# The bias of the float32 attention heads as four rows of their score product

## Chip, cores and metric

The kernel runs on one core of one Trainium2 chip. The metric is the device time of one execution in microseconds (us).

## What is computed

```python
# attention: batch 4, 8 heads, 576 positions, head size 64; x = relu(s)
scores = q @ k.T / sqrt(64)
bias   = -(cum[:, None] - cum[None, :])          # cum = cumsum(max(s, 0)) along the positions
scores = where(causal, -1e9, scores + minimum(bias, 0))
attn   = exp(scores - max) / (sum + 1e-9);  out = attn @ v
# then two feed-forward layers on 2304 tokens, 512 -> 2048 -> 512
x = prelu(x @ w_in, alpha) @ w_out
x = (h * clip(h + 3, 0, 6) / 6) @ w_out2, with h = x @ w_in2
```

Below the diagonal `cum` never falls, so the bias of query row i and key column j is `cum[j] - cum[i]`, and it can be added in the score product itself.

## The kernel before

Attention of the first 256 positions of a batch and head is a "head" here; the other 320 positions are done later in another form (`Task`). The first two batches (16 heads, as 8 `Pair`s of heads 2i and 2i+1) run ahead of all weights; the third batch (8 heads, pairs 8 to 11) runs between the products of the first feed-forward layer (`moe1`). Only these 24 heads are computed in float32 and only they are touched here. The last batch and all later positions (`Task`, class `Sums`) already hold the sums as four rows of their operands.

The start, `cumulate`: `s` is loaded four times, once for each group of 32 partitions; VectorE clips and scales it, scans it along the positions (the scan also reads a tile of zeros, `zz`, that GpSimd fills), ScalarE rounds it, and VectorE replaces the second and fourth group by what the rounding left out. `cum2` then holds, for all 32 heads, the sums in two parts, once in rows 0 to 63 and once in rows 64 to 127. It is also written to the scratch tensor `cum_d` in HBM (`cum_scratch` in the rows).

While that goes on, `keep_clock` has TensorE multiply a tile of ones, `busy`, ten times into a bank that nothing reads ("unread products"). Two more follow each head's transposes.

A head of a pair, `softmax_a`: two blocks of query rows (128 by 128 keys, 128 by 256 keys) in one PSUM bank `s`. For each block there are three products: `pick` (a column of the identity, so that one head's sums are chosen) against `cum2` for the key's sums; `cum2` against minus `pick` for the query's; and the float32 product of `q` and `k`. The two heads of a pair lie in rows 0 to 63 and 64 to 127 of one tile (`qn`, `kn`), and the products of each use only its 64 rows. VectorE adds the mask and takes the row's extreme (L265), ScalarE takes the exponential (L270), VectorE the reciprocal, GpSimd scales (L274). Then `finish` follows one head behind (`LAG`): three transposes on TensorE (L497), a copy on ScalarE (L498), and the two products with `v` (`pv`, L504 and L505). In a float32 product the trace shows two records of TensorE, in one with rounded operands one.

Each engine works through its own queue in order. The order in the queues is dealt by a scheduler that goes by a model of the instructions' times and by priorities, so an edit at the start can reorder the queues far behind it. All transfers are issued by SyncE (SP), in order; each waits until an earlier one that used the same completion counter has landed. Weights come through it too (`load_unit`, L126: four transfers of 512 KB per unit), and ScalarE, GpSimd and VectorE take each apart into a rounded part and a rest (`split_part`, L146 to L163) before TensorE can use it.

Of the kernel before, what the change touches and what calls it, by code (L numbers as in the profile page):

```python
# [9 lines left out]
F32 = mybir.dt.float32  # L10
F32R = mybir.dt.float32r
AF = mybir.ActivationFunctionType
ALU = mybir.AluOpType
# [33 lines left out]
class Pools:  # L47


    def __init__(self, stack, tc, name, groups, wb=0, side=None):  # L50
        self.of, self.wb, self.cum2, self.sums = {}, wb, None, None
        for i, tags in enumerate(groups):
            pool = stack.enter_context(tc.tile_pool(name=f"{name}{i}", bufs=2, reuse_waits="tile", side=side))
            self.of.update(dict.fromkeys(tags.split(), pool))
# [6 lines left out]
def attention_moe_moe(ctx, tc, qt, kt, qn, kn, vp, s, w_in1, w_out1, alpha, w_in2, w_out2, out):  # L61
# [155 lines left out]
    nc.gpsimd.affine_select(  # L217
        mask[:, MASK:], mask[:, MASK:], pattern=[[-1, P]], compare_op=ALU.is_ge, fill=NEG, base=0, channel_multiplier=1
    )
    pick = const.tile([P, 2, BH], F32R, name="pick")  # L220
    for part in range(4):
        rows = slice(part * BH, (part + 1) * BH)
        for sign in range(2):
            nc.vector.tensor_scalar_mul(pick[rows, sign, :], ident[:BH, :BH], 1.0 - 2.0 * sign)

    def cumulate(pool, first):

        s_sb = pool.tile([P, S], F32, tag="wcv", bufs=WB0, name="s_sb")
        for part in range(4):
            nc.sync.dma_start(s_sb[part * BH : (part + 1) * BH], s)  # L230
        first.load(pool)
        sp = pool.tile([P, S], F32, tag="wcv", bufs=WB0, name="sp")
        nc.vector.tensor_scalar(sp, s_sb, 0.0, 8.0, op0=ALU.max, op1=ALU.mult)
        zz = pool.tile([P, S], F32, tag="wcv", bufs=WB0, name="zz")
        nc.gpsimd.memset(zz, 0.0)
        cum = pool.tile([P, S], F32, tag="wcv", bufs=WB0, name="cum")
        nc.vector.tensor_tensor_scan(cum, sp, zz, initial=0.0, op0=ALU.add, op1=ALU.add)
        cum2 = pool.cum2
        nc.scalar.activation(cum2, cum, AF.Copy)
        for part in (1, 3):  # L240
            rows = slice(part * BH, (part + 1) * BH)
            nc.vector.tensor_tensor(cum2[rows], cum[rows], cum2[rows].bitcast(F32), op=ALU.subtract)
        nc.sync.dma_start(cum_d.rearrange("t b s -> (t b) s"), cum2[:D].bitcast(F32))

    def softmax_a(pool, sides, bh=None, js=None):

        cum2 = pool.cum2

        rows = [(0, slice(0, P), P), (1, slice(P, 3 * P), 2 * P)]
        sc = bank("s")  # L250
        todo = []
        for u, o, w in rows:
            if bh is not None:
                one, minus = (pick[js, sign, bh : bh + 1] for sign in range(2))
                todo.append((sc[:, o], one.to_broadcast([D, P]), cum2[js, :w]))
                todo.append((sc[:, o], cum2[js, u * P : (u + 1) * P], minus.to_broadcast([D, w])))
            todo += [(sc[:, o], q[:, u * P : (u + 1) * P], k[:, :w]) for q, k in sides]
        for i, (dst, lt, r) in enumerate(todo):
            nc.tensor.matmul(dst, lt, r, start=(i == 0), stop=(i == len(todo) - 1))  # L259
        t = pool.tile([P, 3 * P], F32, tag="t", bufs=T0, name="t")  # L260
        m = sm.tile([P, 2], F32, tag="m0", name="m")
        den = sm.tile([P, 2], F32, tag="den", name="den")
        rec = sm.tile([P, 2], F32, tag="rec", name="rec")
        for u, o, w in rows:
            nc.vector.tensor_tensor_reduce(  # L265
                t[:, o], sc[:, o], mask[:, MASK - u * P : MASK + P], scale=-0.125, scalar=BIG,
                op0=ALU.add, op1=ALU.min, accum_out=m[:, u : u + 1],
            )
        for u, o, w in rows:
            nc.scalar.activation(t[:, o], t[:, o], AF.Exp, bias=m[:, u : u + 1], scale=-1.0, accum_out=den[:, u : u + 1])  # L270
        nc.vector.tensor_scalar_add(den, den, 1e-9)
        nc.vector.reciprocal(rec, den)
        for u, o, w in rows:
            nc.gpsimd.tensor_scalar(t[:, o], t[:, o], rec[:, u : u + 1], 1.0, op0=ALU.mult, op1=ALU.mult)  # L274
        return t
# [190 lines left out]
    def keep_clock(busy, n, t=None):  # L466

        hp = bank("h")
        r = busy if t is None else t.bitcast(BF16).rearrange("p (k t) -> p k t", t=2)[:, :, 1]
        for _ in range(n):  # L470
            nc.tensor.matmul(hp[:, : r.shape[1]], busy[:, :P], r, start=True, stop=True)  # L471

    class Pair:


# [2 lines left out]

        def load(self, pool):
            i, self.pool = self.i, pool  # L480
            self.k = pool.tile([P, NA], F32, tag="kraw", bufs=3, name="kraw")
            nc.sync.dma_start(self.k, kn[i, :, :NA])
            self.q = pool.tile([P, NA], F32, tag="qraw", bufs=3, name="qraw")
            nc.sync.dma_start(self.q, qn[i, :, :NA])
            self.v = pool.tile([P, 2, 2, D], F32, tag="vraw", bufs=3, name="vraw")
            for j in range(2):
                nc.sync.dma_start(self.v[:, j], vp[2 * i + j, :, :2, :])

        def scores(self, j):
            js = slice(j * D, (j + 1) * D)  # L490
            return softmax_a(self.pool, [(self.q[js, :], self.k[js, :])], 2 * self.i + j, js)

# [19 lines left out]
    def attention0(pool, pairs, lag, together):  # L512
# [20 lines left out]
                loaded += 1  # L533

        if pairs[0].i == 0:
            keep_clock(pool.busy, 10)
            cumulate(pool, pairs[0])
            loaded = 1
        ahead(1)
# [101 lines left out]

    with ExitStack() as st:
        pool = Pools(st, tc, "att0", ("wcv", "kraw qraw vraw", "t pT"), WB0)
        pool.cum2 = st.enter_context(tc.tile_pool(name="cum2a", bufs=1)).tile([P, S], F32R, name="cum2")
        pool.busy = st.enter_context(tc.tile_pool(name="busy", bufs=1)).tile([P, 512], BF16, name="busy")
        nc.gpsimd.memset(pool.busy, 1.0)
        att = attention0(pool, [Pair(i) for i in range(H)], LAG, 0)
        attend(att, 2 * H + 1, pool)
    with ExitStack() as st:
# [11 lines left out]

        with ExitStack() as st2:
            pool2 = Pools(st2, tc, "atta", ("kraw qraw vraw", "t pT"))
            pool2.cum2 = st2.enter_context(tc.tile_pool(name="cum2b", bufs=1)).tile([P, NA], F32R, name="cum2")
            for j in range(2):
                nc.sync.dma_start(pool2.cum2[j * D : (j + 1) * D].bitcast(F32), cum_d[:, :, :NA].rearrange("t b s -> (t b) s"))
            att = attention0(pool2, [Pair(i) for i in range(H, H + H // 2)], LAG, 1)
            done = 0
            while f < A2_OF:
                sb1()  # L670
                if f >= A2_AT:
                    attend(att, LAG + 1 + (f - A2_AT) * H // (A2_OF - A2_AT))
            next(att, None)
# [139 lines left out]
```

## Time and profile before

| | |
|---|---|
| median of 3 runs | 1041.73 us (1041.44 to 1043.83) |
| profiled execution | 1042.1 us, its span 1040.3 us |
| TensorE (PE) busy | 1023.4 us, 98% |
| ScalarE (ACT), VectorE (DVE), GpSimd (POOL) busy | 597.7, 542.9, 376.8 us |
| first score product, first weight product, end of the third batch's heads | 8.1, 63.4, 157 us |

The chain of waits follows the work that ended last back to the start; a piece of it is time that nothing else could have filled without a change of order. A busy PE is not a PE at its best: records overlap, and their ends are modelled.

### The profile page before, as it was taken

Reading aid. Unit: us, or ns where it says so; the run is one execution under the profiler, and the core shown is the slowest. Engines: PE = TensorE matmul, PEld = TensorE weight load, DVE = VectorE, ACT = ScalarE, POOL = GpSimd, SP = SyncE. Lnnn points to the kernel's source line nnn. Section 1 sums busy time; section 2 is a strip of 40 time slices with the busy share of each in tenths; the row PEclk is TensorE's granted clock in tenths of the full one; section 3 lists DMA queues with packets and bytes.
Section 4 is the critical chain, followed back from the end, with each engine's and each line's share of the span. In section 5 each row is a group of like instructions: output and inputs, shape, how many; then the busy total and the mean of one; then the engine's idle time right before and its main releaser. Section 6 shows DMA issues by size and latency. Waiting matters only on the chain.

```text
span 1040.3 us, 16822 instructions
## 1 busy us (share of the span) xinstructions
PE 1023.4 (98%) x5930; PEld 878.5 (84%) x5930; DVE 542.9 (52%) x1365; ACT 597.7 (57%) x1326; POOL 376.8 (36%) x515
## 2 busy tenths in 40 slices
PE   8999999899999999999999999999999999999998
PEld 5657788899999998998998888887888888888897
DVE  5468983466666666766664793455422322222222
ACT  4558876877877778787754773565422422322232
POOL 4345745856666666566630540222000000000000
PEclk9999999999999999999999999999999999999999
DMA  5364403302213122213104753300200100000010
GB/s 173 128 222 163 172 1 110 98 27 88 70 50 94 50 74 79 65 50 94 50 13 147 258 196 110 120 1 1 81 1 1 61 1 1 21 21 1 1 41 21
DMA packets 47620, 76.91 MB, mean 74 GB/s; under 512 B 4816, under 2 KB 25520, under 8 KB 47536
## 3 DMA queue, kind: packets, MB, share of 16 engines
q1 hardware_dynamic: 47536, 75.84, 22.5%
q8 instruction: 47, 0.77, 0.3%
q14 instruction: 37, 0.30, 0.1%
HBM read 66.23 MB, written 9.58 MB: 73 GB/s over the span
## 4 chain that ended last, share of the span: by engine, by line
PE 94%; ACT 3%; issue 1%; DMA 1%; DVE 0%; POOL 0%; SPq 0%; ACTq 0%; POOLq 0%; DVEq 0%
PE y L568 19%; PE h L186 19%; PE h L764 19%; PE o L737 13%; PE o L740 6%; PE s L347 4%; PE s L259 4%; PE pt L384 3%; PE pv L409 3%; PE pv L504 1%; PE pt L497 1%; PE h L471 1%; PE pv L505 0%; ACT ks L319 0%; DMA y_scratch<-yt 0%
## 5 line engine op out<-in xcount | busy, mean ns | idle before, releaser
L186 PE MATMUL h<-xhi,wi 128*128 128x256 f32 (+1 forms) x896 | 223.7, 319 | 3.8 <-DVE gt L591 2.2
L764 PE MATMUL h<-yhl,wi 128*128 128x512 f32 (+1 forms) x960 | 213.3, 370 | 0.2
L764 PEld LDWEIGHTS h<-yhl,wi 128*128 128x128 f32 x960 | 169.3, 188 | 34.8 <-DVE gt L767 1.1
L186 PEld LDWEIGHTS h<-xhi,wi 128*128 128x128 f32 x896 | 155.5, 190 | 19.6 <-DVE gt L591 3.1
L568 PE MATMUL y<-gh,wo 128*128 128x256 f32 (+1 forms) x896 | 165.2, 317 | 1.4 <-ACT gh L594 1.0
L766 ACT ACTIVATE gt<-h,three 128x512 f32<-128x512 f32 (+1 forms) x80 | 51.7, 646 | 166.4 <-PE h L764 162.8
L767 DVE SCALAR_TENSOR_TENSOR gt<-gt,h 128x512 f32<-128x512 f32 (+1 forms) x80 | 50.7, 634 | 183.7 <-ACT gt L766 183.3
L737 PE MATMUL o<-wo,gh 128*128 128x512 f32 x576 | 145.8, 391 | 0.1
L568 PEld LDWEIGHTS y<-gh,wo 128*128 128x128 f32 x896 | 133.8, 190 | 13.4 <-ACT gh L594 1.2
L186 PE MATMUL h<-xlo,wi 128*128 128x256 f32 (+1 forms) x448 | 142.3, 318 | 0.0
L737 PEld LDWEIGHTS o<-wo,gh 128*128 128x128 f32 x576 | 106.8, 188 | 22.9 <-ACT gh L770 0.9
L148 POOL TENSOR_SCALAR wcv<-wcv 128x512 f32<-128x512 f32 x64 | 47.2, 746 | 152.4 <-ACT wcv L146 151.3
L568 PE MATMUL y<-gl,wo 128*128 128x256 f32 (+1 forms) x448 | 92.0, 317 | 0.0
L186 PEld LDWEIGHTS h<-xlo,wi 128*128 128x128 f32 x448 | 85.2, 190 | 6.1 <-DVE wcv L156 0.2
L771 DVE TENSOR_TENSOR gl<-gt,gh 128x512 fp32r<-128x512 f32 (+1 forms) x80 | 51.1, 639 | 69.1 <-ACT gh L770 45.6
L359 POOL TENSOR_SCALAR t<-t,rec 128x384 f32<-128x384 f32 (+2 forms) x96 | 65.1, 681 | 60.5 <-DVE rec L358 34.0
L770 ACT ACTIVATE gh<-gt 128x512 fp32r<-128x512 f32 (+1 forms) x80 | 47.3, 591 | 64.0 <-DVE gt L767 32.9
L591 DVE SCALAR_TENSOR_TENSOR gt<-gt,beta,h 128x256 f32<-128x256 f32 (+1 forms) x112 | 61.5, 552 | 39.2 <-ACT gt L590 38.5
L350 DVE CUSTOM_DVE_ANT_0 t<-s,mask 128x384 f32<-128x384 f32 (+2 forms) x96 | 53.8, 563 | 53.7 <-PE pt L384 30.7
L740 PE MATMUL o<-wo,gl 128*128 128x512 f32 x288 | 79.8, 390 | 0.0
L355 ACT ACTIVATE t<-t,m 128x384 f32<-128x384 f32 (+2 forms) x96 | 67.2, 700 | 16.3 <-DVE m L350 15.0
L568 PEld LDWEIGHTS y<-gl,wo 128*128 128x128 f32 x448 | 70.0, 190 | 5.5 <-issue 0.2
(105 smaller groups left out, 1727.5 us busy)
## 6 DMA issues: line engine op xcount, KB each, us to landing
wraw<-in_w_in SPq DMA_DIRECT2D x32, 512.0 KB
wraw<-in_w_out SPq DMA_DIRECT2D x32, 512.0 KB
kraw<-in_kt SPq DMA_DIRECT2D x32, 288.0 KB
qraw<-in_qt SPq DMA_DIRECT2D x32, 160.0 KB
vraw<-in_vp SPq DMA_DIRECT2D x32, 160.0 KB
y_scratch<-yt SPq DMA_DIRECT2D x18, 256.0 KB
yr<-y_scratch SPq DMA_DIRECT2D x4, 1024.0 KB
out<-ot SPq DMA_DIRECT2D x16, 256.0 KB
```

Source lines behind the costliest of these rows:

```text
L186: nc.tensor.matmul(dst, lt, r, start=first and i == 0, stop=last and i == len(terms) - 1)
L350: nc.vector.tensor_tensor_reduce(t[:n, a:e], sc[:n, : e - a], mask[:n, MASK + n - (e - a) :][:, : e - a] if e == w else mask[:n, : e - a], ...
L355: nc.scalar.activation(t[:n, :w], t[:n, :w], AF.Exp, bias=m[-1][:n], scale=-1.0, accum_out=den[:n])
L359: nc.gpsimd.tensor_scalar(t[:n, :w], t[:n, :w], rec[:n], 1.0, op0=ALU.mult, op1=ALU.mult)
L568: nc.tensor.matmul(ys[dc // per][:, o : o + n], which[:, dc * P : (dc + 1) * P], gg, start=(f == 0 and which is wl and dc % per == 0), sto ...
L591: nc.vector.scalar_tensor_tensor(gt, gt, beta[:, f : f + 1], hp[:, :n], op0=ALU.mult, op1=ALU.add)
L737: nc.tensor.matmul(op[i], lt[:, tsl], r, start=(f == 0 and r is wh), stop=False)
L740: nc.tensor.matmul(op[i], gl[:, tsl], wh, start=False, stop=(f == FC - 1))
L764: nc.tensor.matmul(hp[:, :n], lt, r, start=(i == 0), stop=(i == len(terms) - 1))
L766: nc.scalar.activation(gt[:, :n], hp[:, :n], AF.Relu, bias=three)
L767: nc.vector.scalar_tensor_tensor(gt[:, :n], gt[:, :n], 6.0, hp[:, :n], op0=ALU.min, op1=ALU.mult)
L771: nc.vector.tensor_tensor(gl[:, :n], gt[:, :n], gh[:, :n].bitcast(F32), op=ALU.subtract)
```

## The change

The two bias products of a head are left out for pairs 2 to 11; pairs 0 and 1 keep them. From pair 2 on each head lies in rows 4 to 67 of its own half of a tile, and rows 0 to 3 hold the sums: `k` has the two parts of `cum` in rows 0 and 1 and -1 in rows 2 and 3, `q` has 1 in rows 0 and 1 and the two parts in rows 2 and 3. Three pairs of such tiles stand in turn (`Rows`); GpSimd fills rows 0 to 3 once, and with each pair two further transfers bring the sums from `cum_d`. `q` and `k` are loaded from `qt` and `kt` for it, head by head. `pick` moves to a pool of the first stage and is filled by GpSimd instead of VectorE, and the unread products ahead of the first scores are 18 instead of 10. The copy of `cum2` for the third batch is gone.

```diff
@@ Pools
-        self.of, self.wb, self.cum2, self.sums = {}, wb, None, None
+        self.of, self.wb, self.cum2, self.pick, self.sums = {}, wb, None, None, None
@@ before cumulate
-    pick = const.tile([P, 2, BH], F32R, name="pick")
-    for part in range(4):
-        rows = slice(part * BH, (part + 1) * BH)
-        for sign in range(2):
-            nc.vector.tensor_scalar_mul(pick[rows, sign, :], ident[:BH, :BH], 1.0 - 2.0 * sign)
@@ cumulate, after the scan
+        for part in range(4):
+            rows = slice(part * BH, (part + 1) * BH)
+            for sign in range(2):
+                nc.gpsimd.tensor_scalar(pick[rows, sign, :], ident[:BH, :BH], 1.0 - 2.0 * sign, 1.0, op0=ALU.mult, op1=ALU.mult)
         nc.scalar.activation(cum2, cum, AF.Copy)
@@ new
+    R = 4
+    class Rows:
+        def __init__(self, pool, n):
+            self.tiles = []
+            for i in range(n):
+                k = pool.tile([P, 2, NA], F32, name=f"kr{i}")
+                q = pool.tile([P, 2, NA], F32, name=f"qr{i}")
+                nc.gpsimd.memset(k[:R], -1.0)
+                nc.gpsimd.memset(q[:R], 1.0)
+                self.tiles.append((k, q))
@@ Pair.load
-            self.k = pool.tile([P, NA], F32, tag="kraw", bufs=3, name="kraw")
-            nc.sync.dma_start(self.k, kn[i, :, :NA])
-            self.q = pool.tile([P, NA], F32, tag="qraw", bufs=3, name="qraw")
-            nc.sync.dma_start(self.q, qn[i, :, :NA])
+            if i < 2:
+                self.k = pool.tile([P, NA], F32, tag="kraw", name="kraw")
+                nc.sync.dma_start(self.k, kn[i, :, :NA])
+                self.q = pool.tile([P, NA], F32, tag="qraw", name="qraw")
+                nc.sync.dma_start(self.q, qn[i, :, :NA])
+            else:
+                self.k, self.q = pool.rows.tiles[i % 3]
+                both = slice(2 * i, 2 * i + 2)
+                nc.sync.dma_start(self.k[R : R + D], kt[both, :D, :NA].rearrange("j d n -> d j n"))
+                nc.sync.dma_start(self.q[R : R + D], qt[both, :D, :NA].rearrange("j d n -> d j n"))
+                nc.sync.dma_start(self.k[: R // 2], cum_d[:, both, :NA])
+                nc.sync.dma_start(self.q[R // 2 : R], cum_d[:, both, :NA])
@@ Pair.scores
+            if self.i >= 2:
+                return softmax_a(self.pool, [(self.q[: R + D, j], self.k[: R + D, j])])
@@ attention0
-            keep_clock(pool.busy, 10)
+            keep_clock(pool.busy, 18)
@@ first stage
+        pool.rows = Rows(ahead, 3)
@@ third batch
-            pool2.cum2 = st2.enter_context(tc.tile_pool(name="cum2b", bufs=1)).tile([P, NA], F32R, name="cum2")
-            for j in range(2):
-                nc.sync.dma_start(pool2.cum2[j * D : (j + 1) * D].bitcast(F32), cum_d[:, :, :NA].rearrange("t b s -> (t b) s"))
+            pool2.rows = Rows(st2.enter_context(tc.tile_pool(name="rows", bufs=1)), 3)
```

How the queues stand, at three places. GpSimd at the start, before, from the identity to the first head's scaling (`zz` is the scan's tile of zeros):

```order
masks.py:199 AFFINE_SELECT ident_73<-ident_73 128x128
L646 MEMSET busy_122 128x512
L217 AFFINE_SELECT mask_86<-mask_86 128x128
L235 MEMSET zz_149 128x576
L274 TENSOR_SCALAR t_171<-t_171,rec_174 128x128
L274 TENSOR_SCALAR t_171<-t_171,rec_174 128x256
```

And now (`kr0` to `qr2` are the three pairs of tiles):

```order
masks.py:199 AFFINE_SELECT ident_73<-ident_73 128x128
L480 MEMSET kr0_111 4x512
L481 MEMSET qr0_112 4x512
L480 MEMSET kr1_115 4x512
L481 MEMSET qr1_116 4x512
L480 MEMSET kr2_119 4x512
L481 MEMSET qr2_120 4x512
L670 MEMSET busy_126 128x512
L217 AFFINE_SELECT mask_86<-mask_86 128x128
L236 TENSOR_SCALAR pick_110<-ident_73 32x32 x8
L229 MEMSET zz_161 128x576
```

Six fills stand ahead of `busy`, on which the unread products wait, and these and the eight `pick` operations ahead of `zz`, on which the scan waits.

TensorE from the end of the third head's scores, before (`s_262` and `s_293` are the third and fourth head, `t_171` the first head's softmax):

```order
L259 MATMUL s_262<-kraw_157,qraw_159 128x256
L497 MATMUL pt_210<-ident_73,t_171 128x128 x3
L471 LDWEIGHTS busy_122
L471 MATMUL h_215<-t_171,busy_122 128x384
L471 LDWEIGHTS busy_122
L471 MATMUL h_215<-t_171,busy_122 128x384
L259 MATMUL s_293<-cum2_118,pick_91 128x128
```

And now, from the end of the fourth head's (`t_191` is the first head's softmax, `kr2` and `qr2` are pair 2):

```order
L256 MATMUL s_313<-kraw_177,qraw_179 128x256
L518 MATMUL pt_230<-ident_73,t_191 128x128
L256 MATMUL s_352<-kr2_119,qr2_120 128x128
L256 MATMUL s_352<-kr2_119,qr2_120 128x256
L256 MATMUL s_379<-kr2_119,qr2_120 128x128
L256 MATMUL s_379<-kr2_119,qr2_120 128x256
L518 MATMUL pt_230<-ident_73,t_191 128x128 x2
```

Four heads' scores instead of three now precede the first transpose, and both heads of pair 2 stand between the first transpose and the second.

SP around the write of the sums, before (`wraw` are weights):

```order
L482 DMA kraw_202<-in_kn 128x256
L243 DMA cum_scratch<-cum2_118 64x576
L484 DMA qraw_204<-in_qn 128x256
L487 DMA vraw_206<-in_vp 128x128 x2
L126 DMA wraw_218<-in_w_in1 128x2x512
L126 DMA wraw_220<-in_w_out1 128x1024
```

And now:

```order
L500 DMA kr2_119<-in_kt 64x2x256
L501 DMA qr2_120<-in_qt 64x2x256
L506 DMA vraw_226<-in_vp 128x128 x2
L126 DMA wraw_238<-in_w_in1 128x2x512
L126 DMA wraw_240<-in_w_out1 128x1024
L241 DMA cum_scratch<-cum2_109 64x576
L126 DMA wraw_242<-in_w_in1 128x2x512
L126 DMA wraw_244<-in_w_out1 128x1024
L500 DMA kr0_111<-in_kt 64x2x256
L501 DMA qr0_112<-in_qt 64x2x256
L500 DMA kr1_115<-in_kt 64x2x256
L502 DMA kr2_119<-cum_scratch 2x2x256
```

The write stands behind the first two weight transfers, and pair 2's rows are read back behind two more and three loads of `q` and `k`.

## Rows read from the trace of the kernel before

**Rows 1.** The page, part 4: share of the span by engine.

```profile
PE 94%; ACT 3%; issue 1%; DMA 1%; DVE 0%; POOL 0%; SPq 0%; ACTq 0%; POOLq 0%; DVEq 0%
```

**Rows 2.** Chain in order of time, 0 to 230: start us, us, what.

```profile
8.08 5.73 PE s L259 x22
...
15.28 3.74 PE s L259 x15
...
21.96 2.43 PE s L259 x8
...
34.50 0.62 PE h L471 x2
...
40.94 1.30 PE s L259 x8
...
48.54 0.68 PE h L471 x4
...
53.09 0.57 PE pv L504 x2
53.88 0.48 PE pt L497 x3
...
77.61 1.30 PE s L259 x8
```

**Rows 3.** Timeline of the start: start us, us, engine, line [idle before].

```profile
1.70 0.53 POOL L646 MEMSET busy<- 128x512 bf16 x1
...
2.28 4.45 PE L471 MATMUL h<-busy 128*128 128x512 bf16 x10 [2.28 <-POOL busy L646]
...
2.40 0.58 POOL L235 MEMSET zz<- 128x576 f32 x1
...
5.17 1.36 DVE L237 TENSOR_TENSOR_SCAN cum<-sp,zz 128x576 f32<-128x576 f32 x1
```

**Rows 4.** Timeline of PE, 36 to 42 us: one head's scores.

```profile
38.77 0.32 PE L259 MATMUL s<-cum,pick 64*128 64x128 f32 x1
...
39.05 0.44 PE L259 MATMUL s<-kraw,qraw 64*128 64x128 f32 x2
39.24 0.36 PE L259 MATMUL s<-cum,pick 64*128 64x256 f32 x1
...
39.55 0.59 PE L259 MATMUL s<-kraw,qraw 64*128 64x256 f32 x2
```

**Rows 5.** Stretches: length, busy us of PE, PEld, DVE, ACT, POOL, granted clock, DMA.

```profile
0.00:75.00 75.00, 69.82 (x316) 44.40 (x317) 39.98 (x145) 39.79 (x113) 31.11 (x65) 1.00 0.54 173
75.00:130.00 55.00, 55.00 (x267) 41.93 (x266) 48.77 (x102) 45.33 (x91) 35.07 (x46) 1.00 0.47 170
```

**Rows 6.** Stretches between 470 and 484 us, columns as in the group before.

```profile
475.00:478.80 3.80, 1.93 (x13) 1.12 (x13) 2.27 (x8) 3.73 (x12) 3.35 (x4) 0.99 0.24 60
478.80:482.10 3.30, 3.30 (x14) 3.28 (x15) 1.80 (x10) 3.25 (x10) 2.17 (x4) 0.50 0.39 122
```

**Rows 7.** GpSimd's groups by shape, 0 to 160: busy us, mean ns | idle before.

```profile
L274 POOL TENSOR_SCALAR t<-t,rec 128x128 f32<-128x128 f32 x24 | 12.5, 520 | 37.6 <-DVE rec L272 17.2 <-DVE m L265 9.5 <-PE pv L505 6.0
...
L286 POOL MEMSET kb<- 4x256 f32 x2 | 0.6, 302 | 0.0
...
L104 POOL MEMSET three<- 128x1 f32 x1 | 0.1, 100 | 0.0
```

**Rows 8.** Groups of instructions, 0 to 100 us: ScalarE's part of a head.

```profile
L270 ACT ACTIVATE t<-t,m 128x128 f32<-128x128 f32 (+1 forms) x40 | 17.7, 445 | 8.4 <-DVE m L265 8.3
...
L498 ACT ACTIVATE pT<-pt 128x384 f32<-128x384 f32 x18 | 8.8, 487 | 8.2 <-PE pt L497 8.0
...
L270 ACT ACTIVATION_READ_ACCUMULATOR t<-t,m 128x1 f32 x40 | 7.5, 188 | 0.0
```

**Rows 9.** Timeline, 10 to 19 us: the fourth weight transfer and its first reader.

```profile
11.66 0.47 SPq L126 DMA_DIRECT2D wraw<-in_w_out  x1
...
18.58 0.67 ACT L146 ACTIVATE wcv<-wraw 128x512 f32<-128x512 f32 x1 [0.47 <-DMA wraw<-in_w_out]
```

## What was predicted, before the changed kernel had run

> **What bounds the kernel now.** I read the chain that ended last first: PE carries 94% of the span [rows 1]. So an edit is worth what it takes off PE in the stretch where PE is late, less whatever is late next. The chain in order of time [rows 2] then shows the stage that the change touches. The reader is to compare two pieces of equal work there: one head's eight score records take 2.43 us at 21.96 and 1.30 us at 40.94. Likewise two unread products take 0.62 us at 34.50, while four take 0.68 us at 48.54. Nothing in the kernel differs between these pieces; TensorE runs at the lower of its two levels (1.2 GHz) until about 34.8 us and at the higher (2.4 GHz) from there. The clock column doesn't say so: it reads 1.00 for 0 to 75 us [rows 5], so here the durations decide.
>
> Third comes the start [rows 3]: GpSimd fills `busy` at 1.70, ten unread products run from 2.28 for 4.45 us (0.445 each, the lower level), and PE then stands until the sums are there, at 8.08. The scan starts at 5.17, so 2.91 us pass from its start to the first score product. Last, the granted clock at 475 to 482 us [rows 6]: after 3.8 us in which PE was busy for 1.93, it reads 0.50 for 3.3 us of full work, then 1.00 again. A thin stretch costs the higher level, and dense work brings it back.
>
> **The start.** Six fills of 4x512 now stand ahead of `busy` on GpSimd, eight `pick` operations come over from VectorE, and `zz`, which the scan reads, stands behind them. A fill of 4x256 took 0.302 us [rows 7] and one of 128x576 0.58 [rows 3], so 512 columns take some 0.53: six are 3.2 us. `busy` then ends at 1.70 + 3.2 + 0.53 = 5.4, and the 18 products start there. A 32x32 `pick` operation has no row on GpSimd. It lies between 0.100 us (one column filled) and 0.520 us (the same kind of operation on 128 columns) [rows 7], so eight cost 0.8 to 4.2 us. I take 0.25 each, 2.0, since by columns it is nearer to the small one. With 0.2 for the mask (between the end of `busy`, 2.23, and 2.40 [rows 3]) the scan can start at 5.4 + 0.2 + 2.0 + 0.58 = 8.2 and the scores at 8.2 + 2.91 = 11.1 (9.9 to 13.3). The 18 products end at 5.45 + 8.0 = 13.4 if all run at 0.445, at 11.5 if half of them run at the higher level. I take 11.5: the scores start **3.4 us later** (2 to 5.3). VectorE loses eight small operations; it was waiting there, so that is worth nothing.
>
> **The level.** Ten products in 4.45 us did not raise the clock, and a gap followed. 3.3 us of full work did raise it at 482 [rows 6]. Eighteen products, up to 8 us with no gap to the scores, should. Then the 26.7 us from 8.08 to 34.8, which the chain gives to PE nearly without a break, shrink by 1.30/2.43 to 14.3: **12.4 us less**. The bounds are 0 (not raised) and 13.
>
> **The products removed.** Heads of pairs 2 to 7 (twelve heads) lose both bias products of both row blocks. At the higher level these take, from start to start, 39.05 - 38.77 = 0.28 and 39.55 - 39.24 = 0.31 us [rows 4]: 0.59 of 1.30 per head, 7.1 us in all. The float32 product, with 68 rows for 64, I take at its old price: on 256 columns it shows 0.59 us in two records [rows 4], and `pv`, which contracts 128 rows over 256 columns, also takes two records and 0.57 [rows 2]. Against this stands a loss. Two heads in a row ran partly beside each other while one lay in rows 0 to 63 and the other in 64 to 127: three heads took 5.73 us at 8.08, where three times 2.43 are 7.29, and at 15.28 two took 3.74 instead of 4.86 [rows 2]. From pair 2 on both heads of a pair start at row 0. In the old order only one such meeting lies among them (15.28), so I give back 1.1 x 0.535 = 0.6: **6.5 us less**. The Trainium skill, "TensorE: Matmul & The Clock Gate", Part 3, says that small-K products in distinct row groups run concurrently and gives 3.07 times for four tiles of K=32; two K=64 heads would then by its logic come up to twice as fast as apart. By that rule the merged form would give nothing back wherever heads meet; the rows show 1.3 times, and few meetings.
>
> **New waits.** By now PE needs 4 x 1.30 + 12 x 0.71 for scores and, for 16 heads, 0.48 (transposes) + 0.34 (unread) + 0.79 (`pv`, from 53.09 to 53.88) [rows 2]: 39.5 us from 11.5 on. Two things are late next. (a) PE's queue now has four heads' scores, one transpose, and then pair 2, which needs rows of `cum_scratch`. On SP its write now waits behind two weight loads and for VectorE, two more weight loads follow, and only then come the reads. A weight load issued at 11.66 had landed only at 18.58 [rows 9]; the reads, issued some 3 us after the sums, I expect at 17 to 18, where PE would be ready at 16: 1.8 us (0 to 4). The issues themselves, two more per pair at some 0.47 us each, fit between the pairs. (b) ScalarE spends 2 x (0.445 + 0.188) + 0.487 = 1.75 us per head [rows 8], 28 in all, of 39.8 busy up to 75 us [rows 5]. So it is nearly as full as PE, and waits between the two can't all be hidden. Of PE's 39.5 us I take 10%, 3.9 us (0 to 7). Together **5.7 us more**. GpSimd's six fills for the second batch (3.2 us) stand ahead of weight conversions that are due a dozen us later; I take them at nothing, and at 3 us if they were not hidden.
>
> **The second batch.** Eight heads among the first weight stage lose 0.59 each (one takes 1.30 at 77.61 [rows 2]): 4.7 us. VectorE is busy there for 48.8 of 55 us [rows 5], converting weights, so I count half: **2.4 us less** (0 to 4.7).
>
> **Later stages** keep their work, but the order is dealt anew far down the program: 0, give or take 3.
>
> Sum: 3.4 - 12.4 - 6.5 + 5.7 - 2.4 = -12.2. The profiled execution took 1042.1 us (span 1040.3), 0.4 above the median of the runs, so **1030**; its own range is 1025 to 1036.
>
> **Rivals.** *The level is raised and lost again.* From 12 to 18 us PE has scores for four heads and then waits for the first softmax and pair 2. At 475 a stretch half idle was enough to lose it [rows 6]. Against it: PE here has 3 to 4 of 6 us to do. At the lower level a head costs (0.71 + 1.61)/0.535 = 4.3 for 2.3 us, so three heads until it is back cost 6 us: 1036. The same page of the Trainium skill, Part 4, says that the full clock does not engage for transposes, which don't count as busy the same way; that would favour this rival, since transposes are what PE has then. No row here separates them.
>
> *The weights give it back.* The first weight stage can't run ahead of its conversions; VectorE at 89% [rows 5] becomes the bound, and of the 9.8 us won before it 3 to 5 survive, with nothing of the second batch: 1038. Against it: VectorE is busy for only 40 of the first 75 us.
>
> *Slower: the level isn't raised at all before the weight products.* Place: the unread products, which come 3.1 us later and must do what ten didn't. Then the start costs 3.4, the wait 1.8, and four heads save 4.4 up to 34.8, so PE is about level there; but eight heads follow at 4.3 us each instead of 3.0 at the higher level, 10 us, less 2.4: 1050. It decides from three such heads on; with fewer the removed products pay for it.
>
> *Softmax bounds the heads, and a faster PE only waits.* Then ScalarE's work would set the length. Its 39.8 us up to 75 [rows 5] are what PE needs here, so all of (b), 7 for 3.9: 1033.
>
> **How the numbers follow.** The forecast holds with 0.58, the lost level 0.15, the weights 0.13, not raised 0.08, softmax 0.06. A measurement of this kernel can tell 0.3%, 3.1 us, from no change, so faster is below 1038.6. That gives 0.57 of the forecast, 0.10 of the lost level, 0.06 of the weights and 0.05 of softmax: 0.78. Same gets 0.12, mostly the weights and the lost level; slower 0.10, the third rival and a bad deal of the later order. The range runs from 1022 (early start, little waiting, all of the second batch) to 1041.
>
> **What would show it.** In the changed profile the last unread products should take 0.22 us each, not 0.445; the first score record should stand at 11 to 12; a head of pair 2 or later should take 0.7 us; the first weight products (63 us before) should come at 52 to 55; and the gain should stand by 75 us and grow by some 2 us by 130. The forecast is wrong if records of equal work are twice as long again after 18 us, if GpSimd's fill of `zz` ends after 9.8, or if PE stands for more than 4 us ahead of the first product of pair 2.

## The result, and the profile after

| | us |
|---|---|
| before, beside the changed kernel | 1042.78 median of 4 (1041.44 to 1044.06) |
| changed kernel | 1027.97 median of 4 (1027.47 to 1029.26) |
| ratio | 0.986, 95% interval 0.9842 to 0.9878 |
| changed kernel, profiled | 1028.13, span 1026.4 |

1030 was forecast, 1022 to 1041; the change is 14.8 us faster where 12.2 was said. In the later series the executions of the kernel before, five slow ones near 1053 left out, fall into two groups, near 1035.7 and between 1041 and 1045, and the four beside the changed kernel were all of the upper group. So 14.8 is the gain over that group; over the lower one it is some 8, and over both together the changed kernel's ratio was 0.9891 (0.9853 to 0.993), some 11 us. Below, kernels are compared with one another by their medians, and the kernel before stands for its upper group. The changed kernel gave 1028.0 and 1028.2 in two series.

PE's share of the chain (page, part 4) is 92% where it was 94% [rows 1]:

```profile
PE 92%; ACT 2%; DVE 2%; DMA 1%; POOL 1%; issue 1%; SPq 0%; ACTq 0%; POOLq 0%; DVEq 0%
```

The start of the changed kernel, as [rows 3] (start us, us, engine, line; in brackets the idle time before and what ended it):

```profile
4.51 0.51 POOL L670 MEMSET busy<- 128x512 bf16 x1
...
5.08 6.40 PE L468 MATMUL h<-busy 128*128 128x512 bf16 x18 [5.08 <-POOL busy L670]
...
5.46 1.76 POOL L236 TENSOR_SCALAR pick<-ident 32x32 fp32r<-32x32 f32 x8
...
7.28 0.58 POOL L229 MEMSET zz<- 128x576 f32 x1
...
7.90 1.36 DVE L231 TENSOR_TENSOR_SCAN cum<-sp,zz 128x576 f32<-128x576 f32 x1 [2.55 <-POOL zz L229]
...
9.33 0.15 PEld L468 LDWEIGHTS <-busy 128*128 128x128 bf16 x1 [0.28 <-issue]
...
9.75 1.23 PEld L468 LDWEIGHTS <-busy 128*128 128x128 bf16 x6 [0.28 <-issue]
...
10.78 0.51 SPq L241 DMA_DIRECT2D cum_scratch<-cum  x1
...
11.41 0.32 PE L256 MATMUL s<-cum,pick 64*128 64x128 f32 x1
```

The reader is to see the weight loads of the unread products: one each 0.43 us up to 9.33, then six in 1.23 from 9.75. There the level rises, and the scores start at it, 3.33 us later than before. (As in the kernel before, the clock column reads 1.00 from the start on, so here too the durations decide.) But the level doesn't hold. The same kernel by stretches (length, busy us of PE, PEld, DVE, ACT, POOL, granted clock, DMA share, GB/s), as [rows 5, 6]:

```profile
0.00:75.00 75.00, 62.36 (x298) 40.53 (x299) 45.31 (x153) 44.71 (x127) 45.53 (x91) 0.91 0.63 209
75.00:130.00 55.00, 54.99 (x264) 44.45 (x262) 50.84 (x98) 47.49 (x91) 37.55 (x47) 1.00 0.33 122
...
14.00:16.00 2.00, 1.44 (x14) 1.04 (x13) 0.02 (x2) 1.32 (x4) 0.82 (x2) 1.00 0.94 352
16.00:18.00 2.00, 0.05 (x1) 0.05 (x1) 1.32 (x7) 2.00 (x10) 1.53 (x4) 0.67 1.04 391
18.00:20.00 2.00, 0.43 (x1) 0.13 (x1) 1.99 (x8) 1.89 (x9) 1.82 (x4) 0.50 0.40 96
20.00:26.00 6.00, 5.69 (x20) 4.67 (x21) 4.65 (x19) 3.60 (x14) 5.82 (x9) 0.50 0.23 67
26.00:28.00 2.00, 2.00 (x10) 1.05 (x9) 1.52 (x5) 0.96 (x2) 2.00 (x5) 0.77 0.02 5
...
68.00:70.00 2.00, 2.00 (x5) 1.61 (x6) 1.31 (x6) 2.00 (x8) 1.76 (x4) 0.50 0.82 202
...
475.00:482.00 7.00, 7.00 (x59) 7.00 (x58) 3.69 (x16) 5.26 (x16) 4.54 (x7) 1.00 0.10 28
```

PE does next to nothing from 16 to 20 us, the clock falls to 0.50 and comes back only in 26:28. It is at 0.50 once more at 68:70. At 475, where the kernel before lost it [rows 6], PE is now busy throughout and keeps it. Who is waited for at 16 to 20, first on PE and its weight loads, then on ScalarE, then on SP, then along the chain (start us, us, what), all of the changed kernel:

```profile
14.85 0.59 PE L256 MATMUL s<-kraw,qraw 64*128 64x256 f32 x2
17.95 0.47 PE L518 MATMUL pt<-ident,t 128*128 128x128 f32 x1 [2.51 <-DMA wraw<-in_w_out]
...
17.95 0.18 PEld L518 LDWEIGHTS pt<-ident,t 128*128 128x128 f32 x1 [2.91 <-POOL t L271]
...
20.31 2.90 PE L256 MATMUL s<-kr,qr 68*128 68x128 f32 x8 [1.88 <-DMA kr<-cum_scratch]
```

```profile
13.70 0.67 ACT L146 ACTIVATE wcv<-wraw 128x512 f32<-128x512 f32 x1 [3.73 <-DMA wraw<-in_w_in]
15.05 0.66 ACT L146 ACTIVATE wcv<-wraw 128x512 f32<-128x512 f32 x1 [0.68 <-DMA wraw<-in_w_out]
15.62 0.39 ACT L267 ACTIVATE t<-t,m 128x128 f32<-128x128 f32 x1
```

```profile
15.54 0.33 SPq L502 DMA_DIRECT2D kr<-cum_scratch  x1
15.97 0.25 SPq L503 DMA_DIRECT2D qr<-cum_scratch  x1
...
19.64 0.45 SPq L502 DMA_DIRECT2D kr<-cum_scratch  x1
```

```profile
11.96 7.01 DMA wraw<-in_w_out
...
20.31 2.90 PE s L256 x8
...
30.82 0.66 PE s L256 x4
```

Two things stand behind the weights. On ScalarE it is the first exponential (L267), behind two roundings of weights (L146) that wait 4.4 us for their data. So the first softmax is late, and the transpose at 17.95 waits for it: its weight load names GpSimd's scaling (L271), while the transfer that PE's own row names was only in the middle of landing then. On the way through HBM it is the sums of pair 2. SP issues their two reads, of 4 KB each, at 15.54 and 15.97, behind all four weight transfers, the last of which takes 7.01 us (6.92 before [rows 9]). By the times at which the trace's semaphores count up, the reads land at 19.91 and 20.08, 4.4 and 4.1 us after their issue; PE's row at 20.31 names a read too, but the one issued at 19.64 is pair 4's. PE stands 2.51 + 1.88 = 4.39 us. A head from pair 2 on then takes 0.66 us at the higher level, where eight records took 1.30 [rows 2]. The first weight product (L186) starts at 53.6 us, 9.8 earlier than at 63.4, and the last at 618.5, 13.9 earlier than at 632.4:

```profile
L186 PE MATMUL h<-xhi,wi x896: 274/283/796, 53.6 to 618.5; 128*128 128x256 f32 x128, 128*128 128x512 f32 x52
```

In between something is lost. PE of the changed kernel at the hand-over to the third batch:

```profile
63.18 0.39 PE L186 MATMUL h<-xhi,wi 128*128 128x512 f32 x1
64.58 0.89 PE L256 MATMUL s<-kr,qr 68*128 68x128 f32 x4 [1.01 <-DMA qr<-cum_scratch]
66.48 0.92 PE L256 MATMUL s<-kr,qr 68*128 68x128 f32 x4 [1.01 <-DVE m L262]
67.90 0.80 PE L186 MATMUL h<-xhi,wi 128*128 128x512 f32 x1 [0.49 <-DVE gt L612]
```

The third batch's first heads wait for their rows, PE thins out for four us, and the first weight products after it run at the lower level.

### The profile page after: what moved, and what is told of

It reads as the page before. It is cut to its first block, busy times and chain, and to the rows that moved or that the text cites. A ratio compares the mean times of both kernels' runs of the same rounds, so it can differ in the third digit from the quotient of the medians.

```text
span 1026.4 us, 16686 instructions
## 1 busy us (share of the span) xinstructions
PE 1004.1 (98%) x5858; PEld 866.1 (84%) x5858; DVE 535.6 (52%) x1357; ACT 593.6 (58%) x1326; POOL 389.0 (38%) x535
## 4 chain that ended last, share of the span: by engine, by line
PE 92%; ACT 2%; DVE 2%; DMA 1%; POOL 1%; issue 1%; SPq 0%; ACTq 0%; POOLq 0%; DVEq 0%
PE y L589 19%; PE h L786 19%; PE h L186 19%; PE o L759 13%; PE o L762 6%; PE s L344 4%; PE pv L406 4%; PE pt L381 3%; PE s L256 1%; DMA wraw<-in_w_out 1%; PE pt L518 1%; PE pv L525 1%; ACT t L267 0%; DMA wraw<-in_w_in 0%; DMA qr<-in_qt 0%
## 5 line engine op out<-in xcount | busy, mean ns | idle before, releaser
L186 PE MATMUL h<-xhi,wi 128*128 128x256 f32 (+1 forms) x896 | 225.1, 321 | 2.7 <-DVE gt L612 2.1
L186 PEld LDWEIGHTS h<-xhi,wi 128*128 128x128 f32 x896 | 155.9, 190 | 16.6 <-DVE gt L612 3.6
L186 PE MATMUL h<-xlo,wi 128*128 128x256 f32 (+1 forms) x448 | 142.2, 318 | 0.0
L186 PEld LDWEIGHTS h<-xlo,wi 128*128 128x128 f32 x448 | 85.4, 191 | 6.0 <-issue 0.2
L356 POOL TENSOR_SCALAR t<-t,rec 128x384 f32<-128x384 f32 (+2 forms) x96 | 65.7, 685 | 53.2 <-DVE rec L355 25.8
```

Of the source, the lines that this page charges most:

```text
L186: nc.tensor.matmul(dst, lt, r, start=first and i == 0, stop=last and i == len(terms) - 1)
L356: nc.gpsimd.tensor_scalar(t[:n, :w], t[:n, :w], rec[:n], 1.0, op0=ALU.mult, op1=ALU.mult)
```

## The experiments

**e1_before_18**: the kernel before with the longer run of unread products alone.

```diff
-            keep_clock(pool.busy, 10)
+            keep_clock(pool.busy, 18)
```

> The kernel before with 18 unread products instead of 10, nothing else. Theory: the level is worth most of the first stage's gain. Before, the heads from 8.08 to 34.8 us ran at the lower level, 26.7 us that would be 14.3 at the higher; here no head waits for rows of the scratch tensor, so the level, once raised ahead of the first scores, should hold: 8 to 11 us faster than before, 1032 to 1034, with one head's scores at 1.3 us instead of 2.4 from about 9 us on. Rival 1: the level is lost in the first softmax as in the changed kernel (clock column 0.50 from 17.3 to 27.1 us): 2 to 5 us faster. Rival 2: 18 products from 2.28 us don't raise it at all: 1 to 2 us slower, since the last of them end at 10.3 and the scores wait.

1028.52 us (1027.66 to 1030.85; ratio 0.9883, 0.9844 to 0.9922): as fast as the whole change, and faster than was expected. The level is there from the first scores at 8.5 us, though this kernel too loses it for a while. A rounding of weights on ScalarE (L146) waits 3.33 us for its data, up to 15.48, the exponentials behind it are late, and PE does 0.13 of the next 2 us:

```profile
16.00:18.00 2.00, 0.13 (x1) 0.00 (x0) 0.93 (x6) 2.00 (x9) 1.68 (x4) 0.79 1.05 405
18.00:24.00 6.00, 5.88 (x23) 3.79 (x25) 2.55 (x13) 4.53 (x15) 5.49 (x11) 0.50 0.43 135
```

So the removed products, taken together with what came with them, gave nothing that can be measured. Where they went was the question from here on.

**e2_after_10**: the changed kernel with the old ten products.

```diff
-            keep_clock(pool.busy, 18)
+            keep_clock(pool.busy, 10)
```

> The changed kernel with 10 unread products instead of 18. Theory: in the changed kernel the 18 products buy nothing, because TensorE had done four heads' scores by 15.4 us and then stood until pair 2's rows had landed at 20.3, by which time the higher level was lost again (0.50 from 17.3). At the lower level the four heads take some 3.5 us longer and still end before 20.3: the same time as the changed kernel, within 1 us (1028). Rival: the early level is worth what it saves from 11.4 on: 3 us or more slower (1031 or above).

1032.23 us (1029.58 to 1033.92): the rival was right. In this profile even ten products raise the level, at 8.3 us by the trace's clock records (the last weight load comes 0.35 us after the one at 8.05, where the others lie 0.43 apart), and the first scores run at it; in the kernel before ten did not. But PE stands 1.90 us ahead of these scores, and the level is gone at 11.7 (clock 0.53 from 14 to 26 us). Eight more products are worth 4 us to the changed kernel, where they are worth 14 to the old one; it has less work in the stretch that either level prices, and it loses the level at 16.7 us with 18 products too.

**e3_second_only**: the kernel before, with the new form for pairs 8 to 11 alone.

```diff
+            if i < H:
                 self.k = pool.tile([P, NA], F32, tag="kraw", bufs=3, name="kraw")
...
+            else:
+                self.k, self.q = pool.rows.tiles[i % 3]
...
+            if self.i >= H:
+                return softmax_a(self.pool, [(self.q[: R + D, j], self.k[: R + D, j])])
```

> The kernel before with the change in the second batch of heads alone (pairs 8 to 11 from row tiles of their own, the first 16 heads and the ten unread products as before). Theory: eight heads lose 0.59 us of TensorE each, and TensorE is the bound there, so all 4.7 us come off: 1037 to 1038. Rival (as predicted): VectorE, busy for 48.8 of 55 us there, gives half of it back: 1040. Second rival: the six fills on GpSimd and the transfers of the sums at the hand-over cost what the products save: no change.

1039.36 us (1034.48 to 1043.27), ratio 0.9991 (0.9962 to 1.0019): inconclusive, since the kernel before, beside which it ran, spreads over more than that. In its profile the level rose at 24.7 us, in that of the kernel before at 34.8, with the same start. The stretch that the edit touches is a little shorter: 567.7 us from the first weight product to the layer's last (60.7 to 628.4), where the kernel before takes 569.0, although the level fell once more in it.

**e4_sums_early**: the changed kernel with `pick` filled by VectorE as before, and `busy` ahead of the fills for the rows. (The source has the scan's zeros ahead of the fills too; in the queue they came out behind them, at 5.35 us.)

```diff
+            nc.vector.tensor_scalar_mul(pick[rows, sign, :], ident[:BH, :BH], 1.0 - 2.0 * sign)
...
-                nc.gpsimd.tensor_scalar(pick[rows, sign, :], ident[:BH, :BH], 1.0 - 2.0 * sign, 1.0, op0=ALU.mult, op1=ALU.mult)
...
+        pool.rows = Rows(pool.rowpool, 3)
```

> The changed kernel with pick filled by VectorE at the start, as before, and busy ahead of the six fills on GpSimd. The unread products then start at 2.3 instead of 5.1 us, the sums are there at about 9 instead of 11.4, and the scratch tensor is written ahead of the weights and read back behind one weight transfer instead of four. Theory: the late sums and the wait for pair 2 (15.4 to 20.3 us) and the level lost in it (to 27.1) cost the first stage 2.4 + 3 to 4 + 3.2 us: 5 to 8 us faster than the changed kernel, 1020 to 1023, with the clock column at 1.00 through 20 to 27 us. Rival: from 40 us on the chain runs through weight transfers and their conversion, which don't come earlier: 0 to 2 us faster, 1026 to 1028, with a longer stand of TensorE ahead of the first weight products.

1025.15 us (1021.50 to 1028.23), 2.8 less than the changed kernel by the median, between theory and rival; its six runs spread over both. The scores start at 9.50, but 1.70 us of waiting for VectorE lie ahead of them, and the level falls at 12.1 us while PE is busy:

```profile
10.00:12.00 2.00, 2.00 (x17) 1.65 (x17) 1.18 (x8) 0.76 (x3) 0.00 (x0) 1.00 0.54 121
12.00:14.00 2.00, 2.00 (x14) 2.00 (x14) 0.87 (x7) 1.10 (x6) 0.83 (x2) 0.53 0.81 222
14.00:24.00 10.00, 8.93 (x29) 5.59 (x28) 3.75 (x26) 6.83 (x22) 6.27 (x14) 0.50 0.81 224
```

**c1_weights_later** and **b1_before_18_weights_later**: the first weights four steps later, in the changed kernel and in e1's.

```diff
-W_AT = (2, 14)
+W_AT = (6, 14)
```

> The changed kernel, with the first weights asked for and taken apart four steps later (W_AT 6 instead of 2). Theory: in the changed kernel PE stood from 15.4 to 20.3 us because two weight transfers stood on SP ahead of the reads of the sums, and two roundings of weights (L146, 3.7 us of waiting) on ScalarE ahead of the first exponentials; that gap lost the higher level until 27.1. Without them the first product of pair 2 comes at about 17, the level stays at 1.00 from 10 to 30 us, and the time is 5 to 7 us below the changed kernel's: 1021 to 1023. Rival: the weights are then late for their products (53.6 in the changed kernel), VectorE's conversions become the bound, and what is won before 40 us is given back by 75: 0 to 2 us below, 1026 to 1028, or slower. A second rival: the sums' own way through HBM (write at 10.8, landed by 13) is what is late; then the wait before pair 2 stays above 3 us with nothing of the weights in it.

> The kernel before, with 18 unread products and the first weights four steps later; no bias product is removed. Theory: it holds the higher level from about 8 us on and has no gap at 16 to 18; it beats the kernel before with 18 products (1028.5) by 3 to 5: 1024 to 1026. If the removed products are worth their 6.5 + 2.4 us, the changed kernel with the weights later is 4 to 9 us below this one once its 3.4 us of later start are counted; if it is level with this one, the removed products are hidden or paid back elsewhere. Rival: the weights later cost more than the gap, 1028 to 1031.

1036.85 us (1035.91 to 1038.95) and 1033.95 us (1031.15 to 1035.31): 8.7 and 5.4 slower than their parents. My number for both was wrong, and the first rival right in its direction (b1 is slower than even the rival said, and its trace was not taken apart); the mechanism in the first 40 us came out as said. In c1 pair 2 starts at 15.26, and the clock is 1.00 to 40 us. But its weights were asked for only at 27.9. Their conversions on VectorE then stand among the last heads' softmax, and PE stands 6.69 us for it:

```profile
10.00:20.00 10.00, 9.88 (x68) 7.20 (x66) 7.54 (x42) 6.97 (x29) 4.10 (x10) 1.00 0.39 100
20.00:30.00 10.00, 10.00 (x59) 6.60 (x58) 5.01 (x28) 6.97 (x25) 3.84 (x10) 1.00 0.36 91
50.00:60.00 10.00, 2.38 (x8) 0.99 (x7) 9.80 (x25) 4.61 (x13) 6.08 (x6) 0.50 0.24 96
...
57.65 0.47 PE L518 MATMUL pt<-ident,t 128*128 128x128 f32 x1 [6.69 <-POOL t L271]
```

VectorE is busy for 9.80 of the 10 us in which PE has 2.38: the weights' conversions bound this stretch now, and the first weight product comes at 61.8.

**e6_rows_shared**: one set of row tiles for both batches, so no second fills.

```diff
+    rows0 = Rows(right.enter_context(tc.tile_pool(name="rows0", bufs=1, side="right")), 3)
...
-        pool.rows = Rows(ahead, 3)
+        pool.rows = rows0
...
-            pool2.rows = Rows(st2.enter_context(tc.tile_pool(name="rows", bufs=1)), 3)
+            pool2.rows = rows0
```

> The changed kernel, with one set of the tiles for rows 0 to 3 for both batches: the six fills for the third batch, and the wait for their place, are gone. Theory: at 63.6 to 71.3 us the changed kernel lost some 4 us, since the third batch's reads could be issued only after fills at 57.2, landed at 63, and PE thinned out so that the level fell to 0.50 from 68 to 71.3. Without them PE goes from the heads to the weight products without a break, no clock below 1.00 between 60 and 75, and the time is 2.5 to 4 us below the changed kernel's: 1024 to 1025.5. Rival: the weights and their conversions on VectorE are what is late there (L186 waited 0.49 us for VectorE's L612 at 67.9); then 0, within 1 us of 1028.

1025.39 us (1024.79 to 1026.85), 2.6 less than the changed kernel, as expected, and the clock is 1.00 from 60 to 72 us. The waits there are shorter, not gone:

```profile
64.16 0.92 PE L256 MATMUL s<-kr,qr 68*128 68x128 f32 x4 [0.76 <-DVE m L262]
65.58 0.50 PE L186 MATMUL h<-xhi,wi 128*128 128x512 f32 x1 [0.50 <-DVE gt L612]
```

**b3_combined**: e4's start with the fills last of all, e6's tiles and c1's late weights.

```diff
-W_AT = (2, 14)
+W_AT = (6, 14)
...
+                    nc.gpsimd.tensor_scalar(x[:R].rearrange("p j n -> p (j n)"), zz[:R, : 2 * NA], v, v, op0=ALU.min, op1=ALU.max)
...
+            pool2.rows = rows0[0]
```

> A combination meant to beat both: the changed kernel with pick filled by VectorE as before, the tile of zeros and the unread products ahead of the fills of rows 0 to 3, one set of these tiles for both batches, and the first weights four steps later. Theory: start at 8.5 to 9.5 (2 to 3 us less than the changed kernel), no gap before pair 2 and none at 63 to 71 us, the level held: 1028 - 2.5 - 5 - 3 = about 1017, range 1013 to 1021. Rival: the gains cover the same waits and don't add, the first weight stage goes by its conversions on VectorE: 1021 to 1025.

1035.79 us (1034.18 to 1039.26), a plain miss: it is as slow as c1, with the same late weights (first weight product at 66.4 us), and PE stands 3.96 us for the sums of pair 2. The reads that it waits for are the last of six on SP, issued at 15.66 and 15.98 and landed at 17.64 and 17.82; why the order was dealt so was not taken apart.

**n1_weights_behind_sums, n2_before_weights_behind, o1_weights_behind_only**: the first unit's weights neither ahead of the sums nor at 28 us. GpSimd writes one element of each of the four tiles once the first head's reciprocal is there, and the transfers wait for that. n1 is e6 with it, n2 is e1 (all bias products), o1 the changed kernel with nothing else.

```diff
+        if len(recs) < 8:
+            recs.append(rec)
...
+                if after is not None:
+                    nc.gpsimd.tensor_scalar(t[:1, 0, 0:1].bitcast(F32), after[:1, :1], 1.0, 1.0, op0=ALU.mult, op1=ALU.mult)
                 d = nc.sync.dma_start(t.rearrange(
...
-            units.append(load_unit(w_in1, w_out1, len(units)))
+            units.append(load_unit(w_in1, w_out1, len(units), None if units else recs[0]))
```

> The changed kernel with one set of row tiles (as e6_rows_shared) and the first unit's four weight transfers held until GpSimd has scaled the first head's softmax (some 14.5 us instead of 9.4): GpSimd writes one element of each tile first. They then stand on SP behind the reads of the sums for pairs 2 to 4, and their roundings on ScalarE behind the first four heads' exponentials; unlike c1_weights_later, which asked for them only at 27.9, they land at about 22. Theory (the weights ahead of the sums lose the level and 5 us, while weights at 28 us are too late for their products): pair 2 starts at 15 to 16, clock 1.00 from 10 to 60, first weight products at 46 to 51, 4 to 7 us below e6_rows_shared's 1025.4: 1018 to 1021. Rival: the conversions of the weights bound that stage whatever comes before; then first weight products at 53 or later and 1025 or more.

> The kernel before with 18 unread products and the same hold on the first unit's weights as n1_weights_behind_sums; all bias products are there. Theory: the wait at 16 to 18 us and the lower level at 18 to 24 of e1_before_18 (1028.5) go, 1023 to 1026, and the bias products that n1 lacks are what parts the two: n1 is 3 to 7 us below this one (some 11 us of products, less 3 of later start and what the weights' conversions take back). Rival: the removed products are hidden by the conversions; then n1 and this one are within 2 us of each other.

> The changed kernel with the first unit's weights held until the first head's softmax is scaled (as n1_weights_behind_sums), but with its own second set of row tiles and their six fills. Theory: two separate losses, the weights ahead of the sums (2 to 3 us) and the fills ahead of the third batch (2.6 us by e6_rows_shared), add up to the 5 us between the changed kernel (1028) and n1 (1023.2): then 1025 to 1026.5. Rival: the two losses are one (with the heads early, the fills come due while PE still has heads, or with the fills there, what is won is waited away): 1023 or 1028.

> The changed kernel itself once more, beside o1 on the same chip: 1027.5 to 1029.3 as before, if the numbers of the several series may be compared with each other.

| kernel | us | first weight product |
|---|---|---|
| n1 | 1023.17 (1022.45 to 1024.86) | 50.1 |
| n2 | 1028.16 (1027.40 to 1029.00) | 52.1 |
| o1 | **1021.73** (1021.46 to 1021.88) | 48.9 |
| o2, the changed kernel again | 1028.23 (1027.30 to 1029.76) | 53.2 |

o1 is the fastest here, 6.5 us below the changed kernel on the same chip (ratio to before 0.9825, 0.9791 to 0.9859). In its trace SP reads the sums first. Pair 2's reads are issued at 13.19 and 13.62 and land at 14.88 and 15.13, so they take 1.7 and 1.5 us instead of 4.4 and 4.1: of the 5 us by which they came too late in the changed kernel, half was the later issue and half the longer way beside the weights. PE goes from pair 1 to pair 2 without a gap, and the level holds up to 458 us, where it is lost for a while (clock 0.57 from 458 to 462), much as in the kernel before at 479 [rows 6]. SP, PE and stretches of o1:

```profile
13.19 0.33 SPq L508 DMA_DIRECT2D kr<-cum_scratch  x1
...
16.00 0.41 SPq L128 DMA_DIRECT2D wraw<-in_w_in  x1
```

```profile
15.06 0.33 PE L524 MATMUL pt<-ident,t 128*128 128x128 f32 x1
15.26 0.89 PE L260 MATMUL s<-kr,qr 68*128 68x128 f32 x4
...
58.09 0.89 PE L260 MATMUL s<-kr,qr 68*128 68x128 f32 x4
```

```profile
16.00:18.00 2.00, 2.00 (x16) 1.73 (x15) 1.58 (x10) 2.00 (x9) 1.67 (x5) 1.00 0.55 122
...
68.00:70.00 2.00, 2.00 (x10) 1.66 (x9) 1.34 (x3) 2.00 (x4) 0.00 (x0) 1.00 1.05 414
```

The theory of two losses that add up fell: o1 keeps the second fills and is 1.4 us below n1, which doesn't. The fills cost 2.6 us only where the weights stand ahead of the sums; with the heads on time they are covered: in o1 GpSimd makes them from 52.93 to 55.77 us, and the third batch's first scores, at 58.09, show no wait. Why n1 (from another series, and 2 us above its expected range) is slower than o1 wasn't followed further. n2 against e1 says how much the same hold is worth to a kernel that reads no sums early: 0.4 us, where 2.5 to 5.5 were expected, although n2 keeps the level that e1 loses from 17 to 24 us. The reason is open; it may be in part that e1's order lets two heads' scores run beside each other more often (1.85 us for two at 26.62 and at 38.18, where two apart take 2.60).

n1 is 5.0 below n2, with the higher level all through in both: that is the removed products' own gain, net of a start 1.7 us later. From the first scores to the first weight product n1 takes 39.2 us for 42.9 (the forecast had 6.5 of products less and 3.9 of waiting more), and from there to the layer's last product 563.3 for 566.7 (forecast: 2.4 less).

## Why the prediction came out right, and where it was wrong

The chain of kernels takes the 14.8 us apart: before 1042.8; n2 1028.2 (level held, all products, first scores at 9.19 instead of 8.08); o1 1021.7 (products removed, first scores at 10.90); changed 1028.2 (weights ahead of the sums). What waiting is left in o1 stands in the third row.

| term of the sum | forecast | measured |
|---|---|---|
| later start | +3.4 | +3.33 (8.08 to 11.41) |
| the level, if it holds | -12.4 | -15.7 (before to n2 is -14.6, with 1.1 of later start in it) |
| removed products, with the third batch's | -6.5 - 2.4 = -8.9 | -8.1 (n2 to o1 is -6.4, with 1.7 of later start in it) |
| new waits | +5.7 | +6.0 (o1 to changed is +6.5, with 0.5 of later start in it) |

**Right.** The start came out to 0.1 us, and for the reason given: the scores follow the last unread product at 11.41 (forecast 11.5), while the sums were there at 10.76. The pieces came 0.2 to 0.4 us earlier or shorter than said: `busy` done at 5.02 for 5.4, eight `pick` operations 1.76 for 2.0, `zz` done at 7.86 for 8.2. The last unread products take 1.23 / 6 = 0.21 us, a merged head 0.66 for 0.71. The first weight product comes 9.8 us earlier, which is the forecast's 3.4 - 12.4 - 6.5 + 5.7; but only the sum fits, as the next paragraph shows. Heads side by side: the first two now take 11.41 to 13.33, 1.92 us where twice 1.30 are 2.60, so 1.35 times, as the 1.3 that the prediction read from [rows 2]. The Trainium skill, "TensorE: Matmul & The Clock Gate", Part 3, gives 3.07 times for four tiles of K=32. The estimate that the prediction drew from it, up to twice for two heads of K=64, is not reached here.

**The step that failed is (a) of the new waits.** It was put at 1.8 us, for the sums alone, on SP, with the reads landing at 17 to 18 us. Measured are reads that land at 20.08, 4.39 us of standing, and behind it the rival "raised and lost again", which the forecast held apart at 0.15: the records after 20 us are twice as long, eight of pair 2's in 2.90. Two of the three marks by which the forecast called itself wrong are there. What it missed is two things. One is how long the reads themselves take beside the weights, 4.1 to 4.4 us. The other is ScalarE: [rows 9] shows a rounding of weights waiting for its transfer in the kernel before, and the text used the row for SP only, though in the changed kernel the same instruction stands ahead of the first exponentials. Which of the two costs more was not taken apart; o1 removes both. (b), 3.9 us for a ScalarE nearly as full as PE, did not occur in the changed kernel: from 28.9 us on PE is fully busy. So (a) was too small and (b) too large, and their sum, 5.7, stands beside 6.0 by luck. o1 shows what is left of (b) once (a) is gone: PE is busy for 8.74 and 8.72 of 10 us in 30:40 and 40:50, and its listed waits there are for ScalarE's copies (L525).

**Fills at nothing.** The second batch's fills were costed at 0, and at 3 if not hidden. e6 makes it 2.6 for the kernel as changed, and o1 nothing where the heads are on time.

**The level** was worth 3 us more than forecast in this chain. In the first stage it came out as said: n2's first weight product comes 11.4 us earlier than before (63.4 to 52.1), 12.5 without the 1.1 of later start, where 12.4 was forecast. Another 2.3 us are won up to the layer's last product (632.4 to 618.7); in this stretch n2 keeps the level where the kernel before lost it, at 479 to 482 us [rows 6]. The last us lies between the profiled executions and the medians. All of this is against the upper group of the kernel before, from which the prediction's rows come too; that the four executions beside the changed kernel were of this group is luck. And the argument that ten products don't raise the level and eighteen do is weaker than it read: in e2 ten raised it.

**The rivals.** "Not raised at all" is out. "The weights give it back" is out for the changed kernel, but c1 shows it as the next bound: with the weights four steps later, VectorE's conversions hold up the stage. "Softmax bounds the heads" is out for the changed kernel. For "raised and lost again" the prediction also weighed the transposes. They do run at the higher level here: in the chain of the kernel before three take 0.83 us at 13.81 and 0.48 at 53.88 [rows 2]. Whether they helped to lose it isn't shown: it fell in 2 us in which PE did 0.05 us of work of any kind.

## What to carry to other kernels

A gain in clock level and a gain in work are best tested apart: the eight extra products alone gave the whole of the measured time, while what the removed products won, 6.4 us net of the later start, went into a wait that came with them. When data begins to come through a queue and a scratch tensor, ask what large transfers stand ahead of it on that queue, and which engine has an instruction waiting for those in front of the work on the path; one artificial dependency was worth 6.5 us. And moving a load later is a matter of a few us each way: 16 us won 6.5, 28 us lost 8.7.

## What was not expected of the hardware

- The moment at which the level rises differs from profile to profile: two kernels with the same start show it at 24.7 and at 34.8 us, and in e2 ten unread products raised it at 8.3. That this makes the two groups of the kernel before is likely, not shown.
- PE lost the level while busy, some time after a gap: in e4 the gap was 1.70 us ahead of 9.50, the fall at 12.1; in e2 1.90 us ahead of 10.90, the fall at 11.7. e1 lost it at 17.2, in a gap of some 2 us. It came back at some 27 us in the changed kernel, where PE had been busy since 20.31.
- Beside four weight transfers of 512 KB a read of 4 KB took 4.1 to 4.4 us to land (changed kernel), ahead of them 1.5 to 1.7 (o1). The last weight transfer took 7.01 us in the changed kernel and 6.92 before [rows 9].
